# Loading the shift and scale columns of w_mod: one transfer per norm in place of two

## The chip, the cores and the metric

The kernel runs on one core of a Trainium2 chip, in one launch. The metric is the device time of a launch in microseconds (us), a median over several runs. The profile is one execution taken by the hardware profiler; its times count from the start of its span.

## The reference, cut to what matters

```python
mod = (_silu(c) @ w_mod).reshape(c.shape[0], 6, 1, -1)       # c: 1 x 448, w_mod: 448 x 2688
sa, ca, ga, sb, cb, gb = (mod[:, 0], ..., mod[:, 5])         # six vectors of 448
h = _layernorm(x, axis=-1) * (1 + ca) + sa                   # norm A: shift sa, scale ca
x = x + ga * _A_ref(h, A_wqkv, A_w_phi, A_wo)                # linear attention, gate ga
h = _layernorm(x, axis=-1) * (1 + cb) + sb                   # norm B: shift sb, scale cb
x = x + gb * _B_ref(h, B_w_in, B_w_sp, B_b_sp, B_w_out)      # gated MLP that mixes rows, gate gb
```

x has 2,048 rows of 448 values in bf16. w_mod has six sections of 448 columns, in the order sa, ca, ga, sb, cb, gb. A row of it is 2,688 values, 5,376 bytes, so that the columns of sa and ca lie side by side, and those of sb and cb too.

## The kernel before

The program has two branches; the one that runs is `fast_path`. Its order is written out by hand: `ORDER` (L482 to L533) is a list of words, and the loop at L1243 takes them one by one and records the instructions of the step that each names. A word is `step:arguments@slot/engine`, where the slot is a bank of PSUM. Each engine then runs its own instructions in this order, waiting on semaphores where the data demand it, so a word that comes later never overtakes an earlier one on the same engine.

Rows of x are handled in 16 tiles of 128. The first stage, of some 55 us, has these parts:

- `ld:name/Y` issues one load on SP's queue (`/S`: on ACT's). `wsa`, `wca`, `wsb` and `wcb` (L674 to L677) are the columns of shift A, scale A, shift B and scale B. All four write one buffer, `wm1` (L622), 112 partitions by 4 by 928: shift in columns 0 to 463, scale from 464. Each brings 464 columns, 16 more than a section has, because the matmuls on it read 128 columns at a time from steps of 112. So a load has 448 rows of 928 bytes, 415,744 bytes in all. Since the norms share the buffer, a load for norm B waits until norm A's matmuls have read it.
- `csA`, `ccA`, `csB`, `ccB` (`colform`, L763) are 16 small matmuls each, of a weight load of 112x128 from `wm1` and one column of data: they give a shift or a scale as a column. `esA`, `esB`, `ecA`, `ecB` copy the result out on DVE.
- `SH` and `SC` fold shift and scale into the weights of k, q and v. `kM:i`, `vM:i` (L876, L884) are the matmuls of k and v for tile i, from the transposed normalised rows `hT`.
- `hT` is filled for tiles 0 to 3 by TensorE (`X`, `XE`), and for tiles 4 to 15 by DMA transposes on SP's queue, two tiles each: `T1:a,b` (`turn`, L861), from `xpad`, where `l1a:i` writes tile i on POOL or DVE.
- `ld:wmga`, `ld:wmgb` bring the gates' columns, `ld:wo`, `ld:win1`, `ld:win0`, `ld:wout`, `ld:bsp` weights that later stages use, `ld:x0` to `ld:x5` the rows of x, and `W:t,u` (L1074) transposes blocks of the matrix that mixes rows.

Transfers get eight counters in turn, in the order in which they are recorded (the semaphores DMAHW0 to DMAHW7); one that takes a counter waits until the one eight before it has landed. Whoever uses the data waits on the same counter.

Of the kernel before, what the change touches and what calls it, by code (L numbers as in the profile page):

```python
# [11 lines left out]
BF = mybir.dt.bfloat16  # L12
# [468 lines left out]

ORDER = """  # L482
m5 m1/V ld:wk/S m2a/G m2b/G du:3@3 du:3@1 du:3@2 du:3@4 ld:x0/Y l1s:0 l1e:0,1/G du:3@5 du:3@7 ld:c/S ct@3 FTk:0@6 tbl ce:1 ce:2 ce:3 ce:4 scb FTk:1@2
l1r:0,1 l1a:0/G m3 ld:wq/Y FTq:0@3 ld:x1/Y FTq:1@0 ETk:0/V ld:phi/Y ld:wsa/Y bd/V ETk:1/S PFk:1@6 PFk:3@7 PFk:0@1 ETq:1/V ETq:0/S EPk:3/S PFk:2@4 X:0@3
EPk:0/S EPk:1/V PFq:3@0 EPq:3/S EPk:2/S PFq:2@5 l1s:1 l1e:1,2/G csA@7 esA PFq:1@1 EPq:1/S EPq:2/V PFq:0@2 EPq:0/S ld:wca/Y ccA@6 ld:x2/Y XE:0/S l1r:1,2
SHk@0 ecA SCk:1/S SCk:0/S l1s:2 SCk:2/V l1s:3 l1a:1/G m4 SCk:3/V l1e:2,4/G l1r:2,4 ld:wv/Y SHq@5 SCq:1/V X:1@7 XE:1/S SCq:2/V ld:x3/Y SHv@3 SCv:2/S SCv:0/S
SCv:1/V SCv:3/V SCq:0/S kM:0@2 kF:0 l1s:4 kM:1@0 kF:1 l1s:5 l1s:6 l1s:7 vM:1@3 l1a:3/G X:3@7 XE:3/S kE:0 SCq:3/S kS:0 l1a:2/G vM:0@4 X:2@6 XE:2/S kE:1 vC:0
vC:1 kM:3@5 kF:3 kE:3 l1e:4,8/G l1r:4,8 l1a:6/G vM:3@1 vC:3 l1a:4/G ld:x4/Y l1s:8 kM:2@6 l1a:5/G l1a:7/V m6 l1s:9 ld:wmga/Y gr:0@0 l1s:10 l1s:11 l1e:8,12/G
l1r:8,12 l1a:9/G l1a:11/G l1a:8/G kR:0 kF:2 ld:wcb/Y ld:x5/Y l1s:12 vM:2@7 qM:1@A2 vC:2 ge:0 qM:0@A1 qF:1 kE:2 qE:1 T1:6,8 kM:7@7 vM:6@6 qF:0 T1:4,6 kM:4@1
kP:0/V kS:1 l1s:13 vM:7@4 kR:1 ld:wo/Y l1a:10/V qE:0 kP:1/G kE:4 ld:win1/Y kS:2 kR:2 kF:4 T1:10,12 kM:5@0 kE:5 ld:wsb/Y kP:2/G kM:6@5 kF:5 kE:6 l1s:14 kF:6  # L490
qM:2@A1 qE:2 qF:2 kA:0@A0 l1s:15 l1e:12,16/G l1r:12,16 l1a:14/G l1a:12/G l1a:13/G kS:3 T1:8,10 kR:3 kP:3/V kF:7 ld:wmgb/Y T1:12,14 kS:4 kR:4 l1a:15/G
T1:14,16 kS:5 kR:5 kA:1@A0 kA:2@A0 kA:3@A0 vM:5@5 vC:5 vC:7 kP:4/V kP:5/G kE:7 kS:7 W:0,4 ld:win0/Y wos:1/G vC:6 kM:10@3 W:0,5 kS:6 ld:wout/Y vM:11@2
vM:4@5 vC:4 ccB@7 W:0,0 ld:bsp/Y ecB kM:9@4 kF:9 kE:9 kA:4@A0 kR:7 csB@5 esB W:0,3 kM:8@7 kF:8 kR:6 kE:8 W:0,6 kP:7/V kM:11@4 kF:11 kS:9 kS:8 kP:6/G
# [42 lines left out]
def fast_path(tc, A_x, A_wqkv, A_w_phi, A_wo, B_w_in, B_w_sp, B_b_sp, B_w_out, c, w_mod, out, flag):  # L536
    nc = tc.nc
    S = A_x.shape[1]
# [74 lines left out]
    aph = tc.alloc_tile_pool(name="f_aph", bufs=1)  # L613
# [36 lines left out]
    wmod_v = w_mod.rearrange("(k p) n -> p k n", p=DC)  # L650
# [5 lines left out]
        with nc.allow_non_contiguous_dma(reason="small w_phi blocks"):  # L656
            eng.dma_start(out=phi[:], in_=A_w_phi.rearrange("(g l) d f -> (l d) g f", l=4))

    def load_mod(eng, o, sec):
        eng.dma_start(out=wm1[:, :, o:o + 464], in_=wmod_v[:, :, sec * D:sec * D + 464])  # L660

    LOADS = {
        "c": lambda q: q.dma_start(out=c_row[:], in_=c),
# [15 lines left out]
        "wmgb": lambda q: q.dma_start(out=wmg[:, :, D:2 * D], in_=wmod_v[:, :, 5 * D:6 * D]),
        "wo": lambda q: load_rows(q, wo_s[0:CB], A_wo),  # L680
# [82 lines left out]
    def colform(key, o, slot):  # L763
        t = ps[key] = bank(slot, "cf_ps")
        for m in range(KC):
            for kk in range(KC):
                nc.tensor.matmul(t[:, 0, m:m + 1], lhsT=wm1[:, kk, o + m * CB:o + m * CB + P], rhs=scol[:, kk:kk + 1],
                                 start=(kk == 0), stop=(kk == KC - 1))
# [449 lines left out]
    def hint():  # L1218
# [24 lines left out]
    for word in ORDER.split():  # L1243
        word, _, slot = word.partition("@")
# [59 lines left out]
```

## Time and profile before

| | us |
|---|---|
| median of 3 runs (lowest, highest) | 248.13 (247.74, 248.51) |
| the profiled execution | 248.18 |
| its span | 246.4 |
| PE busy in it | 238.6 |
| DVE, POOL, ACT busy | 184.2, 125.1, 115.5 |

The profiled execution lies 0.05 us above the median. 1.8 us of it are outside the span. Times below are read as "start, length": a row `26.96 0.58 SPq L660` is an issue on SP's queue at 26.96 us that held the queue for 0.58 us. A row of the list of DMA issues ends with the time from issue to landing. In a row of the windows view follow, behind the stretch and its length, the busy time of each engine, PE's granted clock, the mean busy share of the 16 DMA engines (over 1 where packets overlap) and the GB/s that they moved.

### The profile page before, as it was taken

How to read it: one execution, taken by the hardware profiler on the slowest of the kernel's cores; microseconds unless marked ns; L12 is line 12 of the kernel's file. 1: busy time of each engine (PE TensorE's matmuls, PEld its weight loads, DVE VectorE, ACT ScalarE, POOL GpSimd, SP SyncE). 2: the span in 40 equal slices, each digit the busy share in tenths (PEclk: the TensorE clock that was granted, in tenths of full speed). 3: DMA queues.
4: the chain of work that ended last, by engine and by line, in shares of the span. 5: the costliest groups of instructions: out<-in, count | busy, mean ns of one | idle time of the engine just before them, and what ended most of it. 6: DMA issues, size and time to landing. Idle time of an engine off the chain costs nothing.

```text
span 246.4 us, 4186 instructions
## 1 busy us (share of the span) xinstructions
PE 238.6 (97%) x1505; PEld 126.3 (51%) x1513; DVE 184.2 (75%) x371; ACT 115.5 (47%) x232; POOL 125.1 (51%) x174
## 2 busy tenths in 40 slices
PE   7999999999899999999999999999999999999992
PEld 5854566665455555454444444444444544444652
DVE  3899989877998988666568983659989667386552
ACT  2899888749999797888997111000020000000000
POOL 4759986755877976965521059209239400052000
PEclk9999999999999999999999999999999999999999
DMA  7994999950226976543420870009900111000022
GB/s 188 292 284 98 213 272 201 233 141 21 64 67 150 169 133 128 129 88 85 95 33 4 170 130 0 0 3 167 197 19 3 37 56 56 3 0 3 19 71 75
DMA packets 68800, 25.23 MB, mean 102 GB/s; under 512 B 58401, under 2 KB 68642, under 8 KB 68770
## 3 DMA queue, kind: packets, MB, share of 16 engines
q1 hardware_dynamic: 68016, 24.35, 47.0%
q10 hardware_dynamic: 754, 0.52, 0.7%
q8 instruction: 14, 0.23, 0.4%
q14 instruction: 16, 0.13, 0.2%
HBM read 8.87 MB, written 1.84 MB: 43 GB/s over the span
## 4 chain that ended last, share of the span: by engine, by line
PE 92%; DVE 1%; ACT 1%; issue 1%; POOL 1%; DMA 1%; DVEq 0%; POOLq 0%
PE f_psum L1146 29%; PE f_psum L1066 10%; PE f_psum L1036 9%; PE f_psum L1095 8%; PE f_psum L927 6%; PE f_psum L1082 6%; PE f_psum L879 5%; PE f_psum L887 5%; PE f_psum L990 4%; PE f_psum L910 3%; PE f_psum L955 3%; DMA f_x<-in_A_x_dram 1%; PE f_psum L781 1%; ACT f_Eq L932 1%; PE f_psum L786 1%
## 5 line engine op out<-in xcount | busy, mean ns | idle before, releaser
L1146 PEld LDWEIGHTS <-f_z2n 128*128 128x128 bf16 x192 | 18.7, 98 | 22.4
L1146 PE MATMUL f_psum<-f_wsp,f_z2n 128*128 128x512 bf16 x119 | 27.2, 379 | 0.1
L1198 POOL TENSOR_TENSOR f_z1T<-f_gb,f_z1T 128x512 bf16<-128x512 f32 x6 | 8.4, 1411 | 35.8 <-DVE f_gb L1173 35.8
L1036 PE MATMUL f_psum<-f_win,f_hT 112*128 112x448 bf16 (+1 forms) x128 | 26.1, 352 | 0.0
L1066 PE MATMUL f_psum<-f_hT,f_win 112*128 112x512 bf16 x112 | 26.0, 379 | 0.0
L1146 PE MATMUL f_psum<-f_hT,f_Eq 128*128 128x512 bf16 x92 | 22.3, 379 | 0.2
L1166 ACT COPY f_Eq<-f_psum 128x512 f32<-128x512 f32 x4 | 2.3, 585 | 38.6 <-PE f_psum L1146 38.6
L1095 PE MATMUL f_psum<-f_wout,f_z1T 128*128 128x448 bf16 x105 | 20.4, 352 | 0.0
L1069 ACT ACTIVATE f_z1T<-f_psum,f_yb 128x512 bf16<-128x512 f32 x28 | 18.0, 682 | 1.8 <-PE f_psum L1066 1.8
L1036 PEld LDWEIGHTS <-f_hT 112*128 112x128 bf16 (+1 forms) x128 | 12.3, 97 | 11.7
L932 ACT ACTIVATE f_Eq<-f_psum 112x1024 bf16<-112x1024 f32 x16 | 15.9, 1028 | 4.3 <-PE f_psum L927 4.2
L893 DVE TENSOR_REDUCE f_ksum<-f_E 128x32 f32<-128x896 bf16 x16 | 16.8, 1064 | 1.3 <-ACT f_E L882 1.3
L882 ACT ACTIVATE f_E<-f_psum 128x448 bf16<-128x448 f32 x32 | 16.2, 565 | 2.7 <-PE f_psum L879 2.7
L974 DVE TENSOR_TENSOR f_t<-f_psum,f_w 128x896 bf16<-128x896 f32 x16 | 16.9, 1086 | 0.5
L1066 PEld LDWEIGHTS <-f_win 112*128 112x128 bf16 x112 | 10.8, 98 | 12.3
L1040 ACT ACTIVATE f_z2g<-f_psum 128x896 bf16<-128x896 f32 x16 | 14.6, 914 | 4.8 <-PE f_psum L1036 4.0
L900 POOL TENSOR_TENSOR f_phik<-f_E,f_kr 128x896 bf16<-128x896 bf16 x8 | 14.1, 1765 | 4.4 <-DVE f_kr L897 3.6
L1111 DVE TENSOR_TENSOR f_xpad<-f_psum,f_x 128x448 bf16<-128x448 f32 x15 | 9.2, 621 | 8.5 <-PE f_psum L1095 8.3
L1146 PEld LDWEIGHTS <-f_Eq 128*128 128x128 bf16 x96 | 9.4, 98 | 11.3
L1095 PEld LDWEIGHTS <-f_z1T 128*128 128x128 bf16 x105 | 10.2, 98 | 9.4
L927 PE MATMUL f_psum<-f_hT,f_Wq 113*128 113x512 bf16 (+1 forms) x64 | 15.0, 378 | 0.0
L887 PE MATMUL f_psum<-f_wv,f_hT 113*128 113x448 bf16 (+1 forms) x64 | 14.5, 352 | 0.0
(213 smaller groups left out, 498.1 us busy)
## 6 DMA issues: line engine op xcount, KB each, us to landing
out_dram<-f_xpad SPq DMA_DIRECT2D x15, 112.0 KB, 1.8
f_wm<-in_w_mod_dram SPq DMA_DIRECT2D x4, 406.0 KB, 6.5
f_win<-in_B_w_in_dram SPq DMA_DIRECT2D x2, 784.0 KB, 7.2
f_x<-in_A_x_dram SPq DMA_DIRECT2D x3, 448.0 KB, 7.9
f_wmg<-in_w_mod_dram SPq DMA_DIRECT2D x2, 392.0 KB, 7.6
f_wout<-in_B_w_out_dram SPq DMA_DIRECT2D x1, 784.0 KB, 9.4
f_bsp<-in_B_b_sp_dram SPq DMA_DIRECT2D x1, 512.0 KB, 6.2
f_wk_raw<-in_A_wqkv_dram ACTq DMA_DIRECT2D x1, 392.0 KB, 4.1
```

The source lines that it names most:

```text
L882: nc.scalar.activation(out=Er[i % NR][:, s, :], in_=ps["k" + str(i)][:, 0, 0:D], func=ACT.Exp, scale=1.0 - 2.0 * s)
L887: nc.tensor.matmul(t[:, 0, 0:D], lhsT=hT[0:KR[m], i, m, :], rhs=wv[0:KR[m], m, :], start=(m == 0), stop=(m == KC - 1))
L893: nc.vector.tensor_reduce(out=ksum[:, i], in_=Er[i % NR][:].rearrange("p s (c f h) -> p (s c) h f", c=4, h=HP), axis=AX.X, op=ALU.add)
L927: nc.tensor.matmul(t[:, u, :], lhsT=Wq[0:KR[m], m, cc * CB:cc * CB + P], rhs=hT[0:KR[m], 4 * st:4 * st + 4, m, :], start=(m == 0), stop=(m ...
L932: nc.scalar.activation(out=Eq[st // 2][0:CB, 2 * c2:2 * c2 + 2, s, (st % 2) * 512:(st % 2 + 1) * 512], in_=ps["q" + str(n)][0:CB, :, :], f ...
L974: nc.vector.tensor_tensor(out=tr[i % 2][:], in0=numv(i)[:, :, :, 0:DH], in1=wr[i // 2 % 2][:, i % 2].unsqueeze(3).to_broadcast([P, 2, H, D ...
L1036: nc.tensor.matmul(t[:, hf, 0:D], lhsT=hT[0:KR[m], i, m, :], rhs=win_s[0:KR[m], m, FH + hf * D:FH + (hf + 1) * D], start=(m == 0), stop=(m ...
L1066: nc.tensor.matmul(t[:, 0, :], lhsT=win_s[0:CB, m, fc * P:(fc + 1) * P], rhs=hT[0:CB, 4 * st:4 * st + 4, m, :], start=(m == 0), stop=(m == ...
L1069: nc.scalar.activation(out=stage_b()["z1T"][:, fc, st * 512:(st + 1) * 512], in_=ps["y%d_%d" % (st, fc)][:, 0, :], func=ACT.Gelu_apprx_tan ...
L1082: nc.tensor.matmul(g[:, 0, 0:b - a], lhsT=later["z2n"][:, s_, fc * P:(fc + 1) * P], rhs=wspT[t][:, s_, a:b], start=(s_ == 0), stop=(s_ == ...
L1095: nc.tensor.matmul(ps["o" + str(t)][:, 0, 0:D], lhsT=later["z1T"][:, fc, t * P:(t + 1) * P], rhs=wout_s[:, fc, :], start=(fc == 0), stop=( ...
L1146: nc.tensor.matmul(t[:, 0, :], lhsT=b[:, j, f * P:(f + 1) * P], rhs=a[:, j, :], start=(PSTART[k] and j == 0), stop=(j == NH - 1), skip_gro ...
```

## The change

The two loads of a norm become one. `wm1` is 112 partitions by 4 by 912 now, and `load_mod` fills all of it: 448 rows of 1,824 bytes, 817,152 bytes, where the two loads before brought 831,488. `ld:wma` stands where `ld:wsa` stood, and `ld:wca`, which stood before `ccA`, is gone. `ld:wmb` stands where `ld:wsb` stood, and `ld:wcb`, which stood ahead of `ld:x5`, is gone. The scale's columns start at 448. No other word of `ORDER` moves.

```diff
-... ETk:0/V ld:phi/Y ld:wsa/Y bd/V ETk:1/S ...
+... ETk:0/V ld:phi/Y ld:wma/Y bd/V ETk:1/S ...
-... EPq:2/V PFq:0@2 EPq:0/S ld:wca/Y ccA@6 ld:x2/Y ...
+... EPq:2/V PFq:0@2 EPq:0/S ccA@6 ld:x2/Y ...
-... kR:0 kF:2 ld:wcb/Y ld:x5/Y l1s:12 ...
+... kR:0 kF:2 ld:x5/Y l1s:12 ...
-... T1:10,12 kM:5@0 kE:5 ld:wsb/Y kP:2/G ...
+... T1:10,12 kM:5@0 kE:5 ld:wmb/Y kP:2/G ...
-    wm1 = aph.tile([DC, KC, 928], BF, name="f_wm1")
+    wm1 = aph.tile([DC, KC, 2 * D + 16], BF, name="f_wm1")
-    def load_mod(eng, o, sec):
-        eng.dma_start(out=wm1[:, :, o:o + 464], in_=wmod_v[:, :, sec * D:sec * D + 464])
+    def load_mod(eng, sec):
+        eng.dma_start(out=wm1[:], in_=wmod_v[:, :, sec * D:(sec + 2) * D + 16])
-        "wsa": lambda q: load_mod(q, 0, 0),
-        "wca": lambda q: load_mod(q, 464, 1),
-        "wsb": lambda q: load_mod(q, 0, 3),
-        "wcb": lambda q: load_mod(q, 464, 4),
+        "wma": lambda q: load_mod(q, 0),
+        "wmb": lambda q: load_mod(q, 3),
-        "csA": lambda slot: colform("csA", 0, slot), "ccA": lambda slot: colform("ccA", 464, slot),
-        "csB": lambda slot: colform("csB", 0, slot), "ccB": lambda slot: colform("ccB", 464, slot),
+        "csA": lambda slot: colform("csA", 0, slot), "ccA": lambda slot: colform("ccA", D, slot),
+        "csB": lambda slot: colform("csB", 0, slot), "ccB": lambda slot: colform("ccB", D, slot),
```

On SP's queue, the start of the program before the change, from `ld:phi` to `ld:x5` (`f_wm` is `wm1`, `f_wmg` the gates' columns):

```order
L657 DMA f_phi<-in_A_w_phi_dram 112x4x28
L660 DMA f_wm_120<-in_w_mod_dram 112x4x464 x2
L666 DMA f_x<-in_A_x_dram 128x2x448 [waits DMAHW0_49]
L653 DMA f_wv<-in_A_wqkv_dram 112x4x448 [waits DMAHW1_49]
L667 DMA f_x<-in_A_x_dram 128x4x448 [waits DMAHW2_49]
L668 DMA f_x<-in_A_x_dram 128x4x448 [waits DMAHW3_49]
L678 DMA f_wmg<-in_w_mod_dram 112x4x448 [waits DMAHW4_49]
L660 DMA f_wm_120<-in_w_mod_dram 112x4x464 [waits DMAHW7_49,DMAHW5_49,PE_49]
L669 DMA f_x<-in_A_x_dram 128x4x448 [waits DMAHW6_49]
```

The same stretch of SP's queue with the change (lines after L660 have moved up by two):

```order
L657 DMA f_phi<-in_A_w_phi_dram 112x4x28
L660 DMA f_wm_120<-in_w_mod_dram 112x4x912
L666 DMA f_x<-in_A_x_dram 128x2x448
L653 DMA f_wv<-in_A_wqkv_dram 112x4x448 [waits DMAHW0_49]
L667 DMA f_x<-in_A_x_dram 128x4x448 [waits DMAHW1_49]
L668 DMA f_x<-in_A_x_dram 128x4x448 [waits DMAHW2_49]
L676 DMA f_wmg<-in_w_mod_dram 112x4x448 [waits DMAHW3_49]
L669 DMA f_x<-in_A_x_dram 128x4x448 [waits DMAHW4_49]
```

Norm A's pair is one row, norm B's scale is gone from this place, and with one transfer fewer ahead of them the others take the counter before: the load of x's tiles 2 and 3 waits for nothing, and each of the rest for an earlier transfer than it did.

On SP's queue some 20 us later, before the change, from `ld:wo` to the transpose that follows `ld:wmgb` (`f_hT<-f_xpad` are the transposes `T1:10,12`, `T1:8,10` and `T1:12,14`):

```order
L653 DMA f_win<-in_A_wo_dram 112x4x448 [waits DMAHW1_49]
L653 DMA f_win<-in_B_w_in_dram 112x4x896 [waits DMAHW2_49]
L861 DMA_TRANSPOSE f_hT<-f_xpad 128x8x128 [waits DMAHW3_49,DVE_49,Pool_49]
L660 DMA f_wm_120<-in_w_mod_dram 112x4x464 [waits DMAHW4_49]
L861 DMA_TRANSPOSE f_hT<-f_xpad 128x8x128 [waits DMAHW5_49,Pool_49]
L679 DMA f_wmg<-in_w_mod_dram 112x4x448 [waits DMAHW6_49]
L861 DMA_TRANSPOSE f_hT<-f_xpad 128x8x128 [waits DMAHW7_49,Pool_49]
```

The same stretch of SP's queue with the change:

```order
L653 DMA f_win<-in_A_wo_dram 112x4x448 [waits DMAHW7_49]
L653 DMA f_win<-in_B_w_in_dram 112x4x896 [waits DMAHW0_49]
L859 DMA_TRANSPOSE f_hT<-f_xpad 128x8x128 [waits DMAHW1_49,DVE_49,Pool_49]
L660 DMA f_wm_120<-in_w_mod_dram 112x4x912 [waits DMAHW2_49,PE_49]
L859 DMA_TRANSPOSE f_hT<-f_xpad 128x8x128 [waits DMAHW3_49,Pool_49]
L677 DMA f_wmg<-in_w_mod_dram 112x4x448 [waits DMAHW4_49]
L859 DMA_TRANSPOSE f_hT<-f_xpad 128x8x128 [waits DMAHW5_49,Pool_49]
```

The order of the rows is the same; the load of norm B's columns between the first two transposes has grown from 464 to 912 columns.

On PE (TensorE), before the change, the place where `ccB` is followed by `kM:9`, and then, after `kA:4`, by `csB`:

```order
L887 MATMUL f_psum<-f_wv,f_hT 128x448
L767 LDWEIGHTS f_wm_120 [waits DMAHW5_49]
L767 MATMUL f_psum<-f_scol,f_wm_120 128x1 [waits Activation_49]
...
L879 LDWEIGHTS f_hT [waits DMAHW5_49]
L879 MATMUL f_psum<-f_Wk,f_hT 128x448
...
L767 LDWEIGHTS f_wm_120 [waits DMAHW4_49]
```

The same place on PE with the change:

```order
L885 LDWEIGHTS f_hT
L885 MATMUL f_psum<-f_wv,f_hT 128x448
L765 LDWEIGHTS f_wm_120 [waits DMAHW2_49]
L765 MATMUL f_psum<-f_scol,f_wm_120 128x1 [waits Activation_49]
...
L877 LDWEIGHTS f_hT [waits DMAHW3_49]
L877 MATMUL f_psum<-f_Wk,f_hT 128x448
```

PE's instructions stand as before. `ccB` waited for the early load of scale B (counter 5, first use); it waits for the joint load now (counter 2), and `csB` for nothing more. `kM:9` waits for the transpose `T1:8,10` in both, under counter 5 before and 3 now.

More of the change, by code (lines that the diff above doesn't have):

```diff
@@ L483 @@
 m5 m1/V ld:wk/S m2a/G m2b/G du:3@3 du:3@1 du:3@2 du:3@4 ld:x0/Y l1s:0 l1e:0,1/G du:3@5 du:3@7 ld:c/S ct@3 FTk:0@6 tbl ce:1 ce:2 ce:3 ce:4 scb FTk:1@2
-l1r:0,1 l1a:0/G m3 ld:wq/Y FTq:0@3 ld:x1/Y FTq:1@0 ETk:0/V ld:phi/Y ld:wsa/Y bd/V ETk:1/S PFk:1@6 PFk:3@7 PFk:0@1 ETq:1/V ETq:0/S EPk:3/S PFk:2@4 X:0@3
-EPk:0/S EPk:1/V PFq:3@0 EPq:3/S EPk:2/S PFq:2@5 l1s:1 l1e:1,2/G csA@7 esA PFq:1@1 EPq:1/S EPq:2/V PFq:0@2 EPq:0/S ld:wca/Y ccA@6 ld:x2/Y XE:0/S l1r:1,2
-SHk@0 ecA SCk:1/S SCk:0/S l1s:2 SCk:2/V l1s:3 l1a:1/G m4 SCk:3/V l1e:2,4/G l1r:2,4 ld:wv/Y SHq@5 SCq:1/V X:1@7 XE:1/S SCq:2/V ld:x3/Y SHv@3 SCv:2/S SCv:0/S
@@ L487 @@
[L487 to L490, printed above, removed]
+l1r:0,1 l1a:0/G m3 ld:wq/Y FTq:0@3 ld:x1/Y FTq:1@0 ETk:0/V ld:phi/Y ld:wma/Y bd/V ETk:1/S PFk:1@6 PFk:3@7 PFk:0@1 ETq:1/V ETq:0/S EPk:3/S PFk:2@4 X:0@3
@@ new lines @@
+EPk:0/S EPk:1/V PFq:3@0 EPq:3/S EPk:2/S PFq:2@5 l1s:1 l1e:1,2/G csA@7 esA PFq:1@1 EPq:1/S EPq:2/V PFq:0@2 EPq:0/S ccA@6 ld:x2/Y XE:0/S l1r:1,2 SHk@0 ecA
+SCk:1/S SCk:0/S l1s:2 SCk:2/V l1s:3 l1a:1/G m4 SCk:3/V l1e:2,4/G l1r:2,4 ld:wv/Y SHq@5 SCq:1/V X:1@7 XE:1/S SCq:2/V ld:x3/Y SHv@3 SCv:2/S SCv:0/S SCv:1/V
+SCv:3/V SCq:0/S kM:0@2 kF:0 l1s:4 kM:1@0 kF:1 l1s:5 l1s:6 l1s:7 vM:1@3 l1a:3/G X:3@7 XE:3/S kE:0 SCq:3/S kS:0 l1a:2/G vM:0@4 X:2@6 XE:2/S kE:1 vC:0 vC:1
+kM:3@5 kF:3 kE:3 l1e:4,8/G l1r:4,8 l1a:6/G vM:3@1 vC:3 l1a:4/G ld:x4/Y l1s:8 kM:2@6 l1a:5/G l1a:7/V m6 l1s:9 ld:wmga/Y gr:0@0 l1s:10 l1s:11 l1e:8,12/G
@@ L491 @@
+l1r:8,12 l1a:9/G l1a:11/G l1a:8/G kR:0 kF:2 ld:x5/Y l1s:12 vM:2@7 qM:1@A2 vC:2 ge:0 qM:0@A1 qF:1 kE:2 qE:1 T1:6,8 kM:7@7 vM:6@6 qF:0 T1:4,6 kM:4@1 kP:0/V
+kS:1 l1s:13 vM:7@4 kR:1 ld:wo/Y l1a:10/V qE:0 kP:1/G kE:4 ld:win1/Y kS:2 kR:2 kF:4 T1:10,12 kM:5@0 kE:5 ld:wmb/Y kP:2/G kM:6@5 kF:5 kE:6 l1s:14 kF:6
 qM:2@A1 qE:2 qF:2 kA:0@A0 l1s:15 l1e:12,16/G l1r:12,16 l1a:14/G l1a:12/G l1a:13/G kS:3 T1:8,10 kR:3 kP:3/V kF:7 ld:wmgb/Y T1:12,14 kS:4 kR:4 l1a:15/G
```

## The prediction

> **What bounds the kernel now.** I read the page's busy times first, then its chain, then PE's waits.
>
> ```profile
> PE 238.6 (97%) x1505; PEld 126.3 (51%) x1513; DVE 184.2 (75%) x371; ACT 115.5 (47%) x232; POOL 125.1 (51%) x174
> ...
> PE 92%; DVE 1%; ACT 1%; issue 1%; POOL 1%; DMA 1%; DVEq 0%; POOLq 0%
> ```
>
> PE is busy for 238.6 of 246.4 us and makes up 92% of the chain that ended last. So the question is where PE waits, and the list of its waits is short:
>
> ```profile
> PE f_psum L732 <- DVE f_zero L693: 1.2, 1, 1.2
> PE f_psum L955 <- DVE f_t L974: 1.1, 2, 0.7
> PE f_psum L988 <- ACT f_Eq L932: 0.4, 1, 0.4
> PE f_psum L869 <- POOL f_xpad L856: 0.2, 1, 0.2
> ```
>
> None of these is a wait for a transfer, and none for `f_wm`, the buffer that the change touches. Nothing that the two loads cost shows on PE, so their merging has no wait to remove. What it can do is make a wait. In the chain, PE's pieces follow each other without a gap from the first of these two rows to the end of the second, 54.50 us:
>
> ```profile
> 9.13 0.40 PE f_psum L869 x4
> ...
> 52.76 1.74 PE f_psum L927 x8
> ```
>
> So a weight load held up by a late transfer in that stretch is added to the end in full. I therefore ask of each transfer that moves how much room there is between its landing and its first reader.
>
> **The issues that the change touches**, on SP's queue (start, length):
>
> ```profile
> 2.64 1.02 SPq L660 DMA_DIRECT2D f_wm<-in_w_mod_dram  x2
> 4.80 0.41 SPq L666 DMA_DIRECT2D f_x<-in_A_x_dram  x1
> ...
> 11.19 0.33 SPq L660 DMA_DIRECT2D f_wm<-in_w_mod_dram  x1
> 11.56 0.49 SPq L669 DMA_DIRECT2D f_x<-in_A_x_dram  x1
> ...
> 25.68 1.23 SPq L861 DMA_TRANSPOSE f_hT<-f_xpad  x1
> 26.96 0.58 SPq L660 DMA_DIRECT2D f_wm<-in_w_mod_dram  x1
> 27.64 3.53 SPq L861 DMA_TRANSPOSE f_hT<-f_xpad  x1
> 31.22 0.58 SPq L679 DMA_DIRECT2D f_wmg<-in_w_mod_dram  x1
> 32.71 3.08 SPq L861 DMA_TRANSPOSE f_hT<-f_xpad  x2
> ```
>
> **Their readers on PE** are its weight loads. `ccA` is the second `f_wm` row; the third is `ccB`, the row after it `kM:9`.
>
> ```profile
> 9.72 0.50 PEld L767 LDWEIGHTS <-f_wm 112*128 112x128 bf16 x16
> 10.56 0.50 PEld L767 LDWEIGHTS <-f_wm 112*128 112x128 bf16 x16
> ...
> 35.10 0.64 PEld L767 LDWEIGHTS <-f_wm 112*128 112x128 bf16 x16
> 35.66 0.50 PEld L879 LDWEIGHTS <-f_hT 113*128 113x128 bf16 x4
> ```
>
> **Their landings**, from the lists of DMA issues of narrow windows, in order of issue at 3.17 (shift and scale A were issued together from 2.64, this is the second), 26.96 (shift B) and 27.64 us (`T1:8,10`):
>
> ```profile
> f_wm<-in_w_mod_dram SPq DMA_DIRECT2D x1, 406.0 KB, 6.6
> ...
> f_wm<-in_w_mod_dram SPq DMA_DIRECT2D x1, 406.0 KB, 6.4
> ...
> f_hT<-f_xpad SPq DMA_TRANSPOSE x1, 7.3
> ```
>
> Scale A lands at 3.17 + 6.6 = 9.77, shift B at 33.36, `T1:8,10` at 34.94. `kM:9` reads tile 9 at 35.66: **the room there is 0.72 us**, the smallest that I find behind a transfer that moves.
>
> **How fast the longer rows move.** No load of this kernel has rows of 1,824 bytes. Four stretches in which little else moves bound it:
>
> ```profile
> 6.00:8.00 2.00, 1.99 (x33) 1.90 (x31) 1.72 (x6) 0.93 (x2) 1.33 (x2) 1.00 1.12 281
> 26.00:28.00 2.00, 2.00 (x12) 1.06 (x11) 1.93 (x5) 1.80 (x4) 2.00 (x2) 1.00 1.08 252
> 31.50:32.50 1.00, 1.00 (x20) 0.91 (x18) 0.90 (x3) 1.00 (x2) 1.00 (x2) 1.00 1.10 310
> 40.50:41.50 1.00, 1.00 (x8) 0.50 (x6) 0.96 (x3) 1.00 (x4) 0.44 (x1) 1.00 0.95 339
> ```
>
> They are shift A and scale A back to back (281 GB/s), the 1,792-byte rows of `win1` (252), shift B (310), and the 1,792-byte rows of `win0` (339). The same length of row is seen at 252 and at 339, so length alone doesn't settle it. I take 281: it is the nearest, the same bytes of the same tensor by rows of 5,376 bytes, only cut in two.
>
> **Norm B, the term that decides.** Shift B took 415,744 bytes / 310 GB/s = 1.34 us of the queue; the joint load takes 817,152 / 281 = 2.91 us, so what stands behind it on SP's queue moves back by 1.57 us. `T1:8,10` stands right behind it and would land at 34.94 + 1.57 = 36.51, against a weight load at 35.66: PE waits **0.85 us**. The ends: at 339 GB/s the extra is 1.07 and the wait 0.35; at 252 it is 1.90 and the wait 1.18. `ccB` reads the joint load itself, which lands at 33.36 + 1.57 = 34.93 against 35.10: no wait (at 252 GB/s 0.16, which then lies inside that of `kM:9`).
>
> To this comes something that sits in the same microseconds. Around 33.5 two code loads pass on another queue, in the half microsecond from 33.5 to 34.0; and when the next transposes begin (`T1:12,14`), the engines stand nearly still for a while:
>
> ```profile
> q14 instruction: 2, 0.02, 7.7%
> ...
> 35.30:35.80 0.50, 0.50 (x18) 0.48 (x17) 0.50 (x2) 0.32 (x1) 0.50 (x2) 1.00 0.21 37
> ```
>
> 7.7% of 16 engines over 0.5 us are 0.62 us of engine time. I read the gap at 35.3 (37 GB/s) as the other engines of a transpose waiting for one that was held up. With the change the joint load is still moving at 33.5 (31.2 + 2.9 = 34.1), so the transpose that meets the held-up engine would be `T1:8,10`, which PE awaits, not `T1:12,14`. Its cost lies between 0 (the engine catches up) and 0.62; I take half, **0.3 us**, as nothing in the trace tells them apart.
>
> **What follows in that stretch** is late by the same 1.6 to 1.9 us but has more room. `wmgb` and `T1:12,14` come next; the first reader of `T1:12,14` is `kM:12`. `wout` is read first by POOL:
>
> ```profile
> f_hT<-f_xpad SPq DMA_TRANSPOSE x1, 4.2
> ...
> 40.72 0.92 PE L879 MATMUL f_psum<-f_Wk,f_hT 113*128 113x448 bf16 x4
> ...
> f_wout<-in_B_w_out_dram SPq DMA_DIRECT2D x1, 784.0 KB, 9.4
> ...
> 39.09 0.58 SPq L683 DMA_DIRECT2D f_wout<-in_B_w_out_dram  x1
> ...
> 52.48 1.03 POOL L944 TENSOR_TENSOR f_wout<-f_wout,f_g_rep 128x448 bf16<-128x448 bf16 x1 [2.03 <-ACT f_g_rep L941]
> ```
>
> `T1:12,14`, issued at 32.71, lands at 36.9, 3.8 us ahead of 40.72; `wout` lands at 48.5, 4.0 us ahead of 52.48. Both cost nothing while the delay stays under those 3.8 us.
>
> **Norm A.** `csA` needed only shift A before and waits for the whole pair now. The pair carries 14,336 bytes less than the two loads did, so it lands 0.05 us before 9.77, at 9.72, just when the weight load starts: I count **0**. At 252 GB/s (3.24 us in place of 831,488 / 281 = 2.96) it would be 0.28 later and PE would wait that long; at 339 it is early. Since the later wait is measured against a transfer that is not moved by PE, at most a part of the 0.28 would come on top.
>
> **The early issues.** x's tiles 2 and 3 (issued at 4.80, after a wait for `wk`) can be issued some 1.5 us earlier and the last quarter of x (11.56) no longer stands behind scale B's load and its wait for `ccA`. I cost this at nothing in either direction: these transfers stand behind the pair on one queue that is full anyway (1.12 in the row of 6 to 8), and the list of waits has no reader of theirs.
>
> Sum: 0.85 + 0.3 = 1.15 us, on the profiled 248.18: **249.3 us**. The profiled execution is 0.05 us above the median, which is inside the spread of the runs.
>
> **A rule that speaks for the change.** The Trainium skill, page "DMA: Bandwidth & Descriptors", section "Rules for kernel authors", says to join many small transfers into one large one. By the fit on the same page (about 2.0 us and bytes / 436e3 per DMA) the 401,408 bytes more would cost an estimated 0.92 us behind norm B and a wait of 0.2. This trace shows the pair at 281 GB/s, so I don't follow it in the sum; it is the page's form of the first rival.
>
> **The rivals.**
>
> *The long rows are quick and the wait is hidden.* Mechanism: fewer, longer packets move the same bytes faster, as `win0` did at 339 GB/s, and `T1:8,10` moves little. Then PE waits 0.35 us at `kM:9`, and the time is 248.5, not slower by what can be told (0.3%, 0.74 us, is about what a measurement of this kernel can tell from no change). It decides from 1.34 + 0.72 + 0.74 = 2.80 us for the load, that is from 292 GB/s up, without the code loads' share. For it: one of the two stretches with such rows. Against: the other one, and the same bytes at 281.
>
> *The transpose behind a large load stands still.* `T1:10,12`, behind the 784 KB of `win1`, was cut in two by a gap:
>
> ```profile
> 22.50:23.50 1.00, 1.00 (x6) 0.48 (x5) 1.00 (x3) 0.76 (x1) 0.89 (x2) 1.00 1.08 247
> 29.50:31.00 1.50, 1.50 (x15) 0.90 (x14) 1.47 (x3) 0.92 (x3) 1.39 (x2) 1.00 0.64 41
> ...
> q8 instruction: 1, 0.02, 14.5%
> ```
>
> 41 GB/s for 1.5 us, where the transposes of the first row move 247. `T1:8,10` behind 406 KB had no such gap; behind 798 KB it may get one of 1.2 us. That gives 248.18 + 0.85 + 1.2 = 250.2. For it: the size of the load. Against: the last row, a code load between 28.5 and 29.0 (14.5% of 16 engines over 0.5 us, 1.2 us of one engine), explains that gap as well.
>
> *Faster.* With one issue less and x's loads free of two waits, some engine gets ahead and a later wait of PE shrinks. The price is at most the 1.1 + 0.4 us that PE waits for DVE and ACT in the list above, 246.7; it decides only if these engines are late because of a load in the first 20 us, and no row says that.
>
> **Chances.** The forecast (248.9 to 249.9) 0.47; hidden 0.31; the gap 0.16; faster 0.06. Slower by over 0.3%: nearly all of the first and the third, 0.60; faster by over 0.3% 0.06; the rest, 0.34, within. The range goes from 248.2, where the wait is hidden wholly, to 250.6, the gap at 252 GB/s (1.18 + 1.2).
>
> **What would show it.** In the new profile: one row of `f_wm` of 798 KB at 2.64 and one at about 27, and 448 packets fewer for each pair; a wait of PE of 0.8 to 1.5 us before `kM:9` (near 35.7), with `T1:8,10` landing near 36.8; no wait at `csA` beyond 0.3; everything behind 37 us shifted by one and the same amount. I am wrong if `T1:8,10` lands before 36, if PE waits at another place, or if the shift at 37 us is given back later.

## The result, and the profile after

| | us |
|---|---|
| before, median of 6 runs (lowest, highest) | 248.14 (247.52, 248.70) |
| with the change, median of 6 runs | 249.65 (249.12, 250.58) |
| ratio, with its 95% interval | 1.0057 (1.0036 to 1.0078) |

The change makes the kernel slower by 0.6%, some 1.4 us (0.9 to 1.9). The profiled execution of the change took 249.90 us with a span of 248.1, 1.7 us more than the span before.

From the page of the change, the span, the busy times and the packets:

```profile
span 248.1 us, 4186 instructions
...
PE 238.9 (96%) x1505; PEld 126.3 (51%) x1513; DVE 184.4 (74%) x371; ACT 115.6 (47%) x232; POOL 126.0 (51%) x174
...
DMA packets 67872, 25.20 MB, mean 102 GB/s; under 512 B 58369, under 2 KB 67714, under 8 KB 67842
```

PE is busy for about as long (238.9 us, 238.6 before) in a longer span, so most of the 1.7 us are waits. The packets are 928 fewer than the 68,800 of before, among them the forecast 448 for each pair. PE's waits with the change, in the columns engine, line, what it waited for, and us in total, times, longest:

```profile
PE f_psum L730 <- DVE f_zero L691: 1.2, 1, 1.2
PE f_psum L953 <- DVE f_t L972: 1.0, 2, 0.7
PE f_psum L877 <- DMA f_hT<-f_xpad: 0.8, 1, 0.8
PE f_psum L765 <- DMA f_wm<-in_w_mod_dram: 0.7, 1, 0.7
PE f_psum L986 <- ACT f_Eq L930: 0.4, 1, 0.4
```

Two of these rows are new, the third and the fourth, and both are waits for transfers, of which there were none before. Below them the list has 0.3 us for DVE's `f_BD`, also new; the 0.2 for POOL's `f_xpad` of before is gone. Where the two sit is seen in PE's weight loads (start, length; in brackets the idle time before and its releaser): `csA`, then `ccB` and `kM:9`.

```profile
10.45 0.47 PEld L765 LDWEIGHTS <-f_wm 112*128 112x128 bf16 x16 [0.78 <-DMA f_wm<-in_w_mod_dram]
...
35.79 0.64 PEld L765 LDWEIGHTS <-f_wm 112*128 112x128 bf16 x16
37.32 0.49 PEld L877 LDWEIGHTS <-f_hT 113*128 113x128 bf16 x4 [0.89 <-DMA f_hT<-f_xpad]
```

`csA` starts 0.73 us later than before (9.72), `ccB` 0.69 later (35.10), `kM:9` 1.66 later (35.66). So 0.7 us arise at `csA` and stay as they are for 25 us, and some 0.95 are added at `kM:9`. Behind it nothing is added or given back: PE's first matmul on `KVbd`, 19 us further, stands 1.65 us later than before. First the row of before, then that of the change:

```profile
54.52 1.01 PE L955 MATMUL f_psum<-f_KVbd,f_Eq 112*128 112x120 bf16 x16
```

```profile
56.17 1.01 PE L953 MATMUL f_psum<-f_KVbd,f_Eq 112*128 112x120 bf16 x16
```

What stands behind the waits, with the change: the issues on SP's queue, and from the lists of DMA issues of narrow windows the landings of the two joint loads (issued at 2.64 and 27.72).

```profile
2.64 0.49 SPq L660 DMA_DIRECT2D f_wm<-in_w_mod_dram  x1
...
26.39 1.23 SPq L859 DMA_TRANSPOSE f_hT<-f_xpad  x1
27.72 0.53 SPq L660 DMA_DIRECT2D f_wm<-in_w_mod_dram  x1
28.34 3.62 SPq L859 DMA_TRANSPOSE f_hT<-f_xpad  x1
```

```profile
f_wm<-in_w_mod_dram SPq DMA_DIRECT2D x1, 798.0 KB, 7.8
...
f_wm<-in_w_mod_dram SPq DMA_DIRECT2D x1, 798.0 KB, 7.8
```

Norm A's pair lands at 2.64 + 7.8 = 10.44, and `csA` starts at 10.45. Norm B's lands at 35.5, before `ccB` needs it; `T1:8,10` behind it is what `kM:9` waits for.

### The profile page after: what moved, and what is told of

Read it like the earlier page. It is cut to its first block, busy times and chain, and to the rows that moved or that the text cites. A ratio compares the mean times of both kernels' runs of the same rounds, so it can differ in the third digit from the quotient of the medians.

```text
span 248.1 us, 4186 instructions
## 1 busy us (share of the span) xinstructions
PE 238.9 (96%) x1505; PEld 126.3 (51%) x1513; DVE 184.4 (74%) x371; ACT 115.6 (47%) x232; POOL 126.0 (51%) x174
## 4 chain that ended last, share of the span: by engine, by line
PE 65%; DVE 1%; ACT 1%; issue 0%; DVEq 0%
PE f_psum L1144 29%; PE f_psum L1064 10%; PE f_psum L1093 8%; PE f_psum L1034 8%; PE f_psum L1080 6%; PE f_psum L988 3%; PE f_psum L953 1%; PE f_psum L1098 1%; ACT f_z2g L1038 0%; DVE f_t L972 0%; DVE f_v L1014 0%; ACT f_z1T L1067 0%; ACT f_junk L1000 0%; DVE f_xpad L1102 0%; DVE f_v L1017 0%
## 5 line engine op out<-in xcount | busy, mean ns | idle before, releaser
L877 PE MATMUL f_psum<-f_Wk,f_hT 113*128 113x448 bf16 (+1 forms) x64 | 14.3, 352 | 0.8 <-DMA f_hT<-f_xpad 0.8
```

## The experiments

All were timed in five rounds against the kernel before, on one chip for each group of runs. "+us" is what the ratio makes of 248.4 us, with its interval. The last column is the idle time of PE's weight loads ahead of `csA` and `kM:9` in the profiled execution, in us; PE's own wait lists, quoted below, give up to 0.2 less. The first row is the change itself.

| kernel | norm A | norm B | +us (95%) | wait at `csA` / `kM:9` |
|---|---|---|---|---|
| the change | joint | joint, late | 1.4 (0.9 to 1.9) | 0.8 / 0.9 |
| e1_a_joint | joint | two loads | 0.4 (0.0 to 0.8) | 0.5 / 0 |
| e2_b_joint | two loads | joint, late | 0.7 (0.3 to 1.1) | 0 / 0.5 |
| e3_b_two_late | two loads | two loads, both late | 1.0 (0.7 to 1.4) | 0 / 1.0 |
| e4_joint_early | joint | joint, early | 0.5 (0.1 to 0.8) | 0.9 / 0 |
| e5_csA_later | joint, `csA` later | joint, late | 1.0 (0.7 to 1.4) | 0 / 0.6 |
| e6_behind_T1 | joint | joint, behind `T1:8,10` | 2.6 (1.7 to 3.5) | 0.6 / 0, and 1.5 at `ccB` |
| e7_joint_no_wait | joint, `csA` later | joint, early | 0.4 (-0.2 to 1.0) | 0 / 0 |
| e8_phi_first | two loads, other order | two loads | 0.4 (0.1 to 0.7) | 0 / 0 |
| e9_b_half_late | two loads | half of scale B late | 0.3 (-0.1 to 0.7) | 0 / 0 |
| e10_twice | joint | joint, late, done twice | 8.0 (7.6 to 8.5) | 0.8 / 0.4, and 5.4 at `ccB` |
| e11_csA_control | two loads, `csA` later | two loads | 0.0 (-0.3 to 0.2) | 0 / 0 |
| e12_spare | joint | joint, late, and a spare load | 4.8 (3.8 to 5.8) | 0.4 / 2.5 |

### The two norms apart

**e1_a_joint**: the kernel before with norm A's half of the change.

```diff
-... ld:phi/Y ld:wsa/Y bd/V ...     -... PFq:0@2 EPq:0/S ld:wca/Y ccA@6 ...
+... ld:phi/Y ld:wma/Y bd/V ...     +... PFq:0@2 EPq:0/S ccA@6 ...
+    def load_joint(eng, sec):
+        eng.dma_start(out=wm1[:, :, 0:912], in_=wmod_v[:, :, sec * D:(sec + 2) * D + 16])
```

> Norm A's columns in one load, norm B's in two as before. Theory of the two waits: TensorE waits once, at csA, for the joint load, 0.3 to 0.7 us, nothing at kM:9, and the time is 0.3 to 0.7 us above before. Theory of the late start (in the profile of the change x0, wk, wq, x1 and phi, which stand ahead of the joint load, landed 0.2 to 0.6 us later than in that of before, so the wait at csA would be chance): no change, within 0.2 us. Theory of the counters (with one load fewer the later loads are issued earlier and crowd the queue): as the two waits, but with the later loads landing late too.

Measured: 248.94 us against 248.46, ratio 1.0017 (1.0001 to 1.0033). The weight load of `csA`, and the joint load, issued at 2.64:

```profile
9.74 0.47 PEld L769 LDWEIGHTS <-f_wm 112*128 112x128 bf16 x16 [0.52 <-DMA f_wm<-in_w_mod_dram]
```

```profile
f_wm<-in_w_mod_dram SPq DMA_DIRECT2D x1, 798.0 KB, 7.1
```

The load lands at 9.74 and `csA` starts at 9.74. In this execution the load came as early as the prediction had it (9.72), and PE waited all the same, as it was ready 0.52 us earlier. PE's own wait list puts 0.4 of it down to ACT's `f_Wq`, the weight load's row to `f_wm`; the landing at the very start decides for the load. In this execution the wait cost nothing against the profile before: `csA` starts at 9.74 (9.72 there) and `kM:9` at 35.65 (35.66), and its 248.38 us are the lowest of e1's 12 runs. The cost shows in the median alone, and its interval reaches down to 0.0. That norm A costs something by itself rests on e4 as well, which is left with the same wait and is 0.5 us slower (0.1 to 0.8).

**e2_b_joint**: norm B's half alone.

```diff
-... kF:2 ld:wcb/Y ld:x5/Y ...     -... kE:5 ld:wsb/Y kP:2/G ...
+... kF:2 ld:x5/Y ...              +... kE:5 ld:wmb/Y kP:2/G ...
```

> Norm B's columns in one load at the later place, norm A's in two. Theory of the two waits: csA does not wait, kM:9 waits 0.6 to 1.2 us for the transpose T1:8,10, and the time is 0.6 to 1.2 us above before. Theory that the waits are chained (the wait at csA sets the other): no wait at kM:9, within 0.2 us of before.

Measured: 249.41 against 248.46, ratio 1.0029 (1.0013 to 1.0044). PE's wait list has `kM:9`, and a late `w_q` that has nothing to do with the edit:

```profile
PE f_psum L824 <- DMA f_wq_raw<-in_A_wqkv_dram: 0.6, 1, 0.6
PE f_psum L881 <- DMA f_hT<-f_xpad: 0.5, 1, 0.5
```

The wait is a little under the 0.6 to 1.2 that were expected, the time inside. The halves, 0.4 and 0.7 us, make 1.1, and the change 1.4: within their intervals they add up.

### Long rows, or bytes at the later place?

**e3_b_two_late** keeps norm B's two loads with rows of 928 bytes and moves scale B's behind `T1:10,12`.

```diff
-... kF:2 ld:wcb/Y ld:x5/Y ...     -... kE:5 ld:wsb/Y kP:2/G ...
+... kF:2 ld:x5/Y ...              +... kE:5 ld:wcb/Y ld:wsb/Y kP:2/G ...
```

> Norm B's columns in two loads of 928-byte rows, both at the later place; norm A as before. If it is the bytes ahead of T1:8,10 that count: kM:9 waits as with the joint load (e2), within 0.3 us of it, 0.6 to 1.2 us above before. If it is the long rows: no wait at kM:9, within 0.3 us of before.

Measured: 249.42 against 248.46, ratio 1.0041 (1.0027 to 1.0055); `kM:9`:

```profile
36.79 0.49 PEld L879 LDWEIGHTS <-f_hT 113*128 113x128 bf16 x4 [0.98 <-DMA f_hT<-f_xpad]
```

Without one long row and without a merged load, the wait is there. It comes from 415,744 bytes more ahead of `T1:8,10`. The rates of the loads in flight, from the windows of e3 (rows of 928 bytes), and then of the change (rows of 1,824; last two columns: DMA share and GB/s):

```profile
31.50:33.50 2.00, 2.00 (x26) 1.44 (x24) 1.86 (x5) 1.95 (x4) 1.96 (x3) 1.00 1.11 313
```

```profile
6.50:9.50 3.00, 2.73 (x53) 2.65 (x52) 2.78 (x6) 2.38 (x4) 2.28 (x5) 1.00 1.05 266
32.25:34.25 2.00, 2.00 (x24) 1.36 (x22) 1.89 (x4) 1.95 (x4) 1.91 (x4) 1.00 1.05 296
```

Rows twice as long move no faster: 296 GB/s late and 266 early, where the short ones had 310 to 313 and 281. The figures depend on the window: from 31.5 to 33.5 us the joint loads of e2 and e12 have 308 and 305, and from 6.5 to 9.5 us the short rows of the kernel before have 289.

**e4_joint_early** keeps the change but puts norm B's joint load where scale B's load stood.

```diff
-... kF:2 ld:x5/Y ...              -... kE:5 ld:wmb/Y kP:2/G ...
+... kF:2 ld:wmb/Y ld:x5/Y ...     +... kE:5 kP:2/G ...
```

> The change with norm B's joint load moved to where scale B's load stood, ahead of x's last quarter. Two waits: the wait at kM:9 is gone, that at csA stays, 0.3 to 0.7 us above before. Long rows: both stay, as the change (1.5 us above before). If only the later place costs: as before, within 0.2 us.

Measured: 249.15 against 248.46, ratio 1.0019 (1.0004 to 1.0034). One wait for a transfer is left, at `csA`:

```profile
PE f_psum L765 <- DMA f_wm<-in_w_mod_dram: 0.7, 1, 0.7
```

With the 817,152 bytes gone from the place ahead of `T1:8,10`, `kM:9` doesn't wait.

**e9_b_half_late** asks for the point from which the late bytes cost: half of scale B late.

```diff
+        "wcb": lambda q: q.dma_start(out=wm1[:, 0:2, 464:928], in_=wmod_v[:, 0:2, 4 * D:4 * D + 464]),
+        "wcb2": lambda q: q.dma_start(out=wm1[:, 2:4, 464:928], in_=wmod_v[:, 2:4, 4 * D:4 * D + 464]),
-... kE:5 ld:wsb/Y kP:2/G ...
+... kE:5 ld:wcb2/Y ld:wsb/Y kP:2/G ...
```

> The kernel before, with half of scale B's load (two of its four blocks of 112 rows of w_mod, 207,872 bytes in rows of 928 bytes) moved to the late place ahead of shift B; norm A as before. Bytes ahead of T1:8,10: at 281 to 315 GB/s it lands 0.66 to 0.74 us later than in the kernel before, about the 0.72 us of room that kM:9 had there, so PE waits 0 to 0.4 us and the time is 0 to 0.4 us above the kernel before, half or less of what the run with all of scale B late gave (1.0). A fixed price for any further load at the late place: as with all of it, 0.8 to 1.2 us above.

Measured: 248.41 against 248.32, ratio 1.0011 (0.9995 to 1.0027), and `kM:9` runs behind `ccB` without a wait:

```profile
35.05 0.64 PEld L768 LDWEIGHTS <-f_wm 112*128 112x128 bf16 x16
35.61 0.50 PEld L880 LDWEIGHTS <-f_hT 113*128 113x128 bf16 x4
```

207,872 bytes are 0.67 us at 310 GB/s, and the room was read as 0.72. `T1:8,10` lands at 28.09 + 7.3 = 35.39, 0.22 us before `kM:9` reads it. Half of the bytes cost nothing that can be told, all of them 1.0 us. The times alone would allow half of the price for half of the bytes; the profile, with no wait, says that the price begins where the room ends.

### Where the two waits go when work is moved

**e5_csA_later**: the change, with `csA` behind two groups of matmuls that don't need it.

```diff
-... l1e:1,2/G csA@7 esA PFq:1@1 EPq:1/S EPq:2/V PFq:0@2 EPq:0/S ccA@6 ...
+... l1e:1,2/G PFq:1@1 EPq:1/S EPq:2/V PFq:0@2 EPq:0/S csA@7 esA ccA@6 ...
```

> The change, with the step for shift A's column (csA, esA) moved behind the last two matmul groups of the front (PFq:1, PFq:0, some 0.8 us of PE), so that PE has other work while the joint load lands. Two waits: the wait for f_wm in front of csA (0.7 in the change's profile) shrinks to 0.2 or less, the wait of 0.8 to 1.5 for T1:8,10 at kM:9 stays; 0.7 to 1.2 us over the kernel before. Wait only passed on (what PE gains at csA is lost at kM:9, since that transfer doesn't move with PE): 1.2 to 1.7 us over the kernel before, as the change itself. Not the landing of the pair: csA still waits as long, and the time is that of the change.

Measured: 249.49 against 248.47, ratio 1.0041 (1.0027 to 1.0055). The wait list has no `f_wm` any more, and still:

```profile
PE f_psum L877 <- DMA f_hT<-f_xpad: 0.5, 1, 0.5
```

The time is as expected (0.7 to 1.2 over the kernel before); the wait that is left is shorter than the 0.8 to 1.5 expected.

**e11_csA_control**: the same move in the kernel before, where it stands behind two loads.

> The kernel before, with the step for shift A's column (csA, esA) moved behind PFq:1 and PFq:0, as in the two runs that moved it in the change; the loads are as before. A control: if the place of csA by itself costs nothing, the time is within 0.2 us of the kernel before, and the price of the joint loads read from those two runs stands. If it costs or brings 0.3 us or more by itself, that has to be taken off them.

Measured: 248.25 against 248.32, ratio 0.9999 (0.9989 to 1.0009). The place of `csA` costs nothing by itself, so e5 and e7 can be read as they are.

**e7_joint_no_wait**: the change with e4's and e5's moves together.

> The change with both mends: csA and esA behind PFq:1 and PFq:0, and norm B's joint load ahead of x's last quarter, where the load of scale B stood. Two waits: neither the wait for f_wm at csA nor that for T1:8,10 at kM:9 is left above 0.2 us, and the time is within 0.4 us of the kernel before (247.9 to 248.8 if that runs at 248.4). Long rows or one load in place of two cost something besides the waits: 1 us or more over the kernel before, with the waits gone all the same.

Measured: 248.52 against 248.47, ratio 1.0016 (0.9992 to 1.0040). Its wait list has no transfer in it:

```profile
PE f_psum L730 <- DVE f_zero L691: 1.2, 1, 1.2
PE f_psum L953 <- DVE f_t L972: 1.1, 2, 0.7
PE f_psum L986 <- ACT f_Eq L930: 0.4, 1, 0.4
PE f_psum L867 <- ACT f_Wk L824: 0.3, 1, 0.3
```

The medians differ by 0.05 us; one of the 12 executions, with 251.24 us at a mean granted clock of 0.990, widens the interval. With both waits gone the joint loads, their long rows and the turned counters cost nothing that can be told (the interval leaves room for up to 1.0 us), and they bring nothing either.

**e6_behind_T1**: the change with norm B's joint load behind `T1:8,10`.

```diff
-... T1:10,12 kM:5@0 kE:5 ld:wmb/Y kP:2/G ... kS:3 T1:8,10 kR:3 ...
+... T1:10,12 kM:5@0 kE:5 kP:2/G ... kS:3 T1:8,10 ld:wmb/Y kR:3 ...
```

> The change, with norm B's joint load moved on SP's queue from ahead of T1:8,10 to right behind it. The bytes ahead of the transpose: T1:8,10 lands 1.3 us or more ahead of kM:9 and PE doesn't wait there; the joint load now lands 1 to 2 us later than in the change, past the weight load of ccB (35.3 to 36.0), so the wait sits at ccB, 0.5 to 2 us: 0.5 to 2.5 us over the kernel before. The transpose is slow by itself (standing still behind whatever comes): kM:9 still waits 0.5 us or more. Load quick enough: no wait at either place, and 0.3 to 0.7 us over the kernel before, from norm A alone.

Measured: 250.65 against 248.47, ratio 1.0104 (1.0067 to 1.0142). `ccB`, and `kM:9` behind it:

```profile
36.83 0.47 PEld L765 LDWEIGHTS <-f_wm 112*128 112x128 bf16 x16 [1.50 <-DMA f_wm<-in_w_mod_dram]
37.23 0.31 PEld L877 LDWEIGHTS <-f_hT 113*128 113x128 bf16 x3
```

The transpose is in time and the load late: the bytes don't fit ahead of 35 us in either order. The time, 2.6 us over the kernel before, is at the upper end of the 0.5 to 2.5 expected; the two waits of this execution, 0.6 and 1.5, make 2.1, and at 250.01 us it is one of the faster of its six.

**e12_spare**: the change, with 612,864 bytes more behind norm B's load, into a buffer that nothing reads.

```diff
+    wm2 = aph.tile([DC, 3, 2 * D + 16], BF, name="f_spare")
+        "wmx": lambda q: q.dma_start(out=wm2[:], in_=wmod_v[:, 0:3, 3 * D:5 * D + 16]),
-... kE:5 ld:wmb/Y kP:2/G ...
+... kE:5 ld:wmb/Y ld:wmx/Y kP:2/G ...
```

> The change, with one more load right behind norm B's joint load on SP's queue: three quarters of the same columns (612,864 bytes, rows of 1,824 bytes) into a spare buffer that nothing reads and nothing waits for, unlike the run that loaded the same buffer twice. Bytes ahead of T1:8,10, paid in full: at 281 to 315 GB/s it lands 1.95 to 2.2 us later than in the change, PE waits for it at kM:9 and nowhere else, and the time is 1.7 to 2.4 us above the change's, so about 2.9 to 3.8 us above the kernel before. Bytes hidden or given back later: less than 1 us above the change.

Measured: 253.30 against 248.39, ratio 1.0193 (1.0151 to 1.0234), with runs from 250.79 to 254.54. PE's longest wait is at `kM:9`:

```profile
PE f_psum L879 <- DMA f_hT<-f_xpad: 2.4, 1, 2.4
```

The place is as expected, the wait 1.6 us longer than in the change, and the time 1.1 us above what was expected at most. The windows say where that comes from (PE busy is the first number behind the length, the granted clock the third from the end):

```profile
36.25:38.50 2.25, 0.00 (x0) 0.00 (x0) 1.16 (x3) 0.13 (x1) 0.51 (x1) 1.00 1.28 232
40.00:44.00 4.00, 4.00 (x30) 2.23 (x28) 3.06 (x6) 2.10 (x5) 2.84 (x2) 0.57 0.97 206
```

PE stood still from 36.25 to 38.5, and from 40 to 44 its granted clock was 0.57: an estimated 4.0 x 0.43 = 1.7 us of its work are lost there. 253.02 of the profiled run less 1.7 is 251.3, 2.9 above before, which is inside the expectation; the execution of 250.79 had a mean clock of 0.999, the one of 254.54 had 0.982.

**e10_twice** was meant for the same question: norm B's joint load done twice (`ld:wmb/Y ld:wmb/Y`).

> The change, with norm B's joint load done twice at its place (the same 817,152 bytes once more, nothing left out). Bytes ahead of T1:8,10: it lands 2.6 to 2.9 us later than in the change (281 to 315 GB/s), PE waits for all of it as the room is used up already, and the time is 2.4 to 3.0 us above the change's, so 3.6 to 4.6 us above the kernel before; the wait sits at ccB, which reads this load, or at kM:9. Hidden somewhere, or given back later in the program: less than 2 us above the change.

Measured: 256.49 against 248.32, ratio 1.0324 (1.0304 to 1.0344). It missed, as it tested something else:

```profile
27.84 8.19 SPq L660 DMA_DIRECT2D f_wm<-in_w_mod_dram  x2
36.12 1.23 SPq L859 DMA_TRANSPOSE f_hT<-f_xpad  x1
```

```profile
42.00:46.00 4.00, 3.90 (x32) 2.33 (x33) 1.21 (x5) 0.98 (x2) 0.35 (x1) 0.50 1.20 237
46.00:50.00 4.00, 4.00 (x23) 2.12 (x22) 3.27 (x5) 2.16 (x5) 2.49 (x2) 0.73 1.38 237
```

The second load writes the buffer of the first, so it waits on SP's queue until the first has landed, and the issue of `T1:8,10` waits behind it until 36.12 (28.34 in the change). `ccB` waits for the second load, with its weight load idle for 5.39 us until 41.22, and then the clock falls, as in e12: the rows above make an estimated 4.0 x 0.50 + 4.0 x 0.27 = 3.1 us of PE's work lost. So the 8 us are the price of a blocked queue and of the clock behind the long wait, not of bytes alone; e12 takes its place.

### Is the front bound by when small loads land?

**e8_phi_first**: the kernel before with `w_phi` and scale A's load earlier on SP's queue, `w_q` and x's tile 1 behind them.

```diff
-... m3 ld:wq/Y FTq:0@3 ld:x1/Y FTq:1@0 ETk:0/V ld:phi/Y ld:wsa/Y bd/V ETk:1/S ...
+... m3 ld:phi/Y ld:wq/Y FTq:0@3 FTq:1@0 ETk:0/V ld:wsa/Y bd/V ld:wca/Y ld:x1/Y ETk:1/S ...
```

> The kernel before, with only the order of the early loads on SP's queue changed: w_phi ahead of w_q, and scale A right behind shift A, both ahead of x's tile 1. The two loads stay two. Late start (PE's first stage is bounded by when small loads land): w_phi lands some 0.5 us earlier, the waits of 0.3 to 0.5 us for f_BD that several profiles show at the front go, and the time is 0.2 to 0.6 us below the kernel before. Not bounded by them: no difference (within 0.2 us). Rival: w_q or x's tile 1 becomes the late one, with a wait of PE or of DVE for it, and the time is 0.3 to 1 us above.

Measured: 248.91 against 248.47, ratio 1.0017 (1.0004 to 1.0029): slower. The list has no wait for `f_BD`, for which PE waits 0.2 to 0.5 us in several other profiles (0.5 in e1, 0.3 in the change; none in the profile before). The wait for `f_xpad` has grown from 0.2 to 0.5, and one for `w_q` is new:

```profile
PE f_psum L869 <- POOL f_xpad L856: 0.5, 2, 0.3
...
PE f_psum L822 <- DMA f_wq_raw<-in_A_wqkv_dram: 0.3, 1, 0.3
```

My theory fell. Its rival, that `w_q` or x's tile 1 becomes the late one, fits the list and the time but is not shown by it: `w_q` is waited for in e2 and e11 too, 0.6 us in each, where nothing has been put ahead of it. No version here beats the kernel before.

## Why the prediction was right where it was, and where it was not

**What bounds the kernel, and that the merge has no wait to remove**: right. PE's busy time stayed (238.9), and the new waits are in the span in full, 1.65 us at 56.17 and 1.7 at the end.

**Norm B, the joint load ahead of `T1:8,10`**: right in mechanism, place and about in size. e2 (0.7 us) and e3 (1.0) show it alone, e4 and e9 take it away, e6 shows that the wait follows the order. The forecast was 0.85 + 0.3; the waits at `kM:9` in PE's lists are 0.5 in e2 and in e5, 0.8 in the change and 0.9 in e3. The rate came out at 296 GB/s, not 281: 817,152 / 296 = 2.76 us, 1.42 more than shift B's 1.34 (forecast 1.57). The landing, by the start of `kM:9`, came near 37.3 and not near 36.8, as the whole stretch was late in that execution: `T1:8,10` was issued at 28.34, 0.70 after the 27.64 of before. That start varies by itself: `T1:10,12`, issued at 26.39 here and at 25.68 before, was issued at 26.96 in e11, which has no joint load.

**The code loads, 0.3 us**: no run gives the size, and the cause that I named is not borne out. What is there is the gap. In all five profiles with all of norm B's columns ahead of `T1:8,10` (the change, e2, e3, e5, e12) half a microsecond in which the engines move 11 to 40 GB/s stands ahead of `kM:9`; the row is the change's.

```profile
36.25:36.75 0.50, 0.27 (x11) 0.18 (x8) 0.50 (x2) 0.46 (x1) 0.50 (x1) 1.00 0.14 23
```

In the kernel before, e1, e8, e9 and e11, which have half of scale B's columns there or none, such a gap (37 to 40 GB/s) comes 0.3 to 0.5 us after `T1:8,10` has landed. So the transpose that PE awaits does meet the gap now. But the sum doesn't give a price for it: 34.94 + 0.70 + 1.42 is 37.06, and `kM:9` starts at 37.32, 0.26 us later, while the same working puts e2 and e5 each 0.37 us too late (`T1:8,10` issued at 28.43 and 28.24, `kM:9` at 36.78 and 36.59). And the code loads don't keep their distance from the gap: before they pass between 33.5 and 34.0, over 1.2 us ahead of it, in the change between 35.5 and 36.0 (the row below), right ahead of it. What makes the gap stays open; moving code loads by themselves was not tried.

```profile
q14 instruction: 2, 0.02, 7.7%
```

**Norm A, counted as 0**: wrong. This is the term that was mis-sized: e1 gives 0.4 us (0.0 to 0.8), e4 0.5, and the joint load held `csA`'s weight load by 0.36 to 0.86 us in all six profiles that have it at its old place (0.78 in the change, 0.52, 0.86, 0.61, 0.77 and 0.36 in e1, e4, e6, e10 and e12). By the prediction's own sign, a wait of PE at another place, it was wrong here. The step that failed is "just when the weight load starts". I took a landing (9.72) and a start (9.72) of one execution and called the room between them zero. Both ends vary: the joint load landed between 9.74 and 10.54 in those six, and PE was ready between 9.2 and 9.8. A transfer that lands early gives nothing back, and one that lands late holds PE up, so a room of zero on paper is a cost on average. How long `csA` waits in one execution is thus in part chance, as the second theory of e1 had it; that it waits in all six is not. The landing that I built on was an early one. With two loads scale A's landed at 9.77 before, and at 10.87, 10.47, 9.67 and 11.27 in e2, e3, e9 and e11: the joint load comes no later than the second of two. So two loads are not free of waits either: `ccA` waited for scale A's in e2, in the row below, and for 0.36 us in e11. The price of the merge is only what it adds.

```profile
10.91 0.47 PEld L769 LDWEIGHTS <-f_wm 112*128 112x128 bf16 x16 [0.35 <-DMA f_wm<-in_w_mod_dram]
```

What it adds is at `csA`. Before, shift A alone landed at 2.64 + 5.7 = 8.34, and `csA` had 1.4 us of room (0.5 in e2, where it landed at 9.14); the merge used up all of it. My bound of 0.28 was one of the rate alone and left the start out; counted from 9.77 to the reader at 9.72 it would have been 0.33.

**That at most a part of norm A's wait would come on top of norm B's**: not seen. e5, with norm A's wait gone, is at 1.0 us, 0.4 below the change, which is all that norm A costs in e1, though the intervals are as wide as that.

**Later transfers and early issues cost nothing**: right as far as can be told. No row of theirs is in the list of waits, and e7, which has the early issues and the turned counters, is at 0.05 us by the medians, 0.4 (-0.2 to 1.0) by the ratio.

**The rivals.** The quick rows fell as a mechanism: ahead of `T1:8,10` the long rows had 296 to 308 GB/s and the short ones of e3 313. But for the time it was close. The line that the prediction drew for this rival, 292 GB/s, was crossed: at 296 the sum leaves a wait of 2.76 - 1.34 - 0.72 = 0.70 us at `kM:9`, less than the 0.74 that the prediction took for what can be told from no change, and norm B alone, e2, came out at 0.7. The change stands clearly above the kernel before with norm A on top. The gap behind a large load, as a mechanism of 1.2 us, is not there; the gap ahead of `kM:9` is half a microsecond, and e3 has it behind loads of 406 KB. Faster was not seen: e7 has the change's early issues without its waits and is no faster, and the other order of the front that e8 tried is slower.

**The sum** was 249.3 and the time 249.65. Norm B was put at 1.15 us and measured 0.7 to 1.0, norm A was put at 0 and measured 0.4. That the two errors nearly cancel is luck.

**The rule to join many small transfers.** The Trainium skill, page "DMA: Bandwidth & Descriptors", section "Rules for kernel authors": the row is on many small transfers and adds that "under 64 KB you're paying mostly overhead". These runs don't test it at such sizes. They show that it doesn't carry over to loads of 406 KB here: joined to 798 KB they moved no faster, and whoever needed one half waited for both. The page's fit, which gave the prediction 0.92 us for the bytes more, is given there for SWDGE transfers (those that GpSimd issues); on SP's queue the rates above make it 1.42.

## What to carry to other kernels

Before two loads are joined, ask who reads the first half, and how much room there is behind the transfer that follows on the same queue: here the reader of the first half waited for the whole load, and the transpose behind it landed later by what the load had grown. Loads of 406 KB gained nothing by being joined. A room that is read as zero in one execution is likely a cost, since lateness is paid and earliness is not; read it in several executions.

## What the runs showed of the hardware that was not expected

- A wait of PE can cost more than its length. After 2.4 us of wait in e12, the granted clock was 0.57 from 40 to 44 us; after 5.0 us of wait in e10 it was 0.50 from 42 to 46. The Trainium skill, page "TensorE: Matmul & The Clock Gate", section "Part 1: The HAM clock gate (the "warmup" mystery)", names an idle window of about 3.4 us as the condition for half the clock; here a shorter stretch was followed by it, the measurement decides, and why it was enough is open. In the profiled executions of the change, with waits of 0.7 and 0.8 us, and of e6, with one of 1.5 us, it stayed at 1.00.
- The first loads land at other times from execution to execution, whatever the kernel: `w_q`, the second issue on SP's queue, took 5.0 us to land before, 5.5 in the change and 6.0 in e11, and nothing ahead of it differs between the three. A wait read in one profile has that much play.
